# Attention and a Mish MLP on one core: the two row sums of a step are handled one column at a time, and the written-out order is replaced

## The chip, the core and the metric

The kernel runs on one core of a Trainium2 chip. The metric is device time in microseconds (us), the median of several executions. The engines are named as a profile names them: PE is TensorE (matmuls; PEld are its weight loads), DVE is VectorE, ACT is ScalarE, POOL is GpSimd, SP is SyncE, which only starts transfers (DMAs) here. Each works through a queue of its own, in order, and waits for the others by semaphores.

## What is computed

Attention with rotary position embedding over 4 batches of 8 heads, 576 positions, 64 channels, then an MLP with the mish function over all 2304 tokens (512 to 2048 to 512 channels):

```python
scores = scale * np.matmul(q_rot, k_rot.transpose(0, 1, 3, 2))
scores = scores - np.max(scores, axis=-1, keepdims=True)
attn = np.exp(scores)
attn = attn / (np.sum(attn, axis=-1, keepdims=True) + 1e-09)
x = np.matmul(attn, v).transpose(0, 2, 1, 3).reshape(2304, 512)
h = x @ w_in
g = h * np.tanh(np.where(h > 20.0, h, np.log1p(np.exp(np.minimum(h, 20.0)))))
out = g @ w_out
```

## The kernel before

Two heads are a pair P (0 to 15); four pairs are a batch. A pair's 576 query rows are done in steps t of 128 rows, and step 4 of an even pair takes the last 64 rows of two pairs, so there are 72 steps. One step (`step`, L577) runs as follows. `scores` (L475) multiplies on PE into two PSUM pairs, one for each head. `max_exp` (L504) takes the row maximum on DVE (L507) and on ACT the exp with the sum of each row into a column of `sm` (L509): `sm` has two columns, one for each head. `inverse` (L514) adds 1e-9 to both sums and scales them (L517, one instruction over two columns), and takes the reciprocal (L519) into `rs`. The first 18 steps (batch 0, the exact ones) turn e on PE (`turned`, L534: transposes L542, L557, L559, copied out by ACT or DVE). The other 54 steps write weights in two fp16 parts (L523, L525 or L526, on POOL, ACT or DVE; L530 on DVE, which reads e and the first part) and turn them by a DMA on SP's queue. `av` (L606) multiplies by V and leaves the result in two parts in `xt` (L660 to L665).

The rotation of q and k (`rope_turn`, L367) is two multiplies and an add a half tile (L383, L387), on POOL but for the first pair, where DVE shares it. The MLP's weights come as fp64 words and are decoded into two fp16 parts (`decode`, L742: L751 to L771, on ACT, POOL and DVE), after their largest exponent was found (`amax`, L718, and `max_exponent`, L336: a maximum on DVE, L340, a transpose on PE, L343, a maximum, L345, two small operations, L333, a broadcast on PE, L349). The MLP runs in eight chunks of 256 or 320 tokens: `h_unit` (L856; matmuls L873, mish L878), `h_split` (L882; L888 or L889, then L892) and `p_sub` (L896; matmuls L909, eviction L917 or L918, store).

The order of all this is not found when the program is built: `ORDER` (L59) lists every operation by its number in the plan, and each engine's queue is that list's rows for that engine. A letter behind the number (b, c) picks the second or third engine that an operation may run on; `@` gives its PSUM banks; `+n` puts n fills ahead of it (L1022: matmuls of the identity matrix with itself into a bank that is about to be overwritten, which compute nothing and keep PE busy). The durations written in the calls of `op` serve the search that made the list; when the kernel is built they have no effect. In batch 0 ahead of the first MLP product the weights of w_in are decoded beside the steps; the first such product (L873) stands behind pair 3's second step.

Of the kernel before, what the change touches and what calls it, by code (L numbers as in the profile page):

```python
# [18 lines left out]
ALU = mybir.AluOpType  # L19
# [40 lines left out]
    59 58 3 5 2 11 6 4 92 137b 108 20 107 119 32 109 131c 12 7 110@0 19 8b 111 112 113 114@1+3 13 115 116 14 118@2 9  # L60
    15 159 136@3 10b 125b 120 64@45+10 25 23 124@0 138 45 121 63 21 65 62 67 66 156 16b 68 139 130@1 78@45+5 69 24 126
    70 22 132 71@2 79 26 72 38 81 80 61 75@3+6 158 60 82 29 157 140 85@4+5 127 27 86 133 73@2+4 77 201b 170 141 28 134
    93@54+5 160 122 17b 169 76 195b 123 87@0 33 83 171 88 94 172@1 30 161@3 189b 173 84 95 174 42 96 89@0+4 175 162 97
    176@1 163 135 177 117 128 164 142@54+3 98 178 229 194@3 129 74 165@1 196 90 91 224@2 39 166 180 145 188@0 181 143
    183b 517 146 228 43 144 40 225 240b 190 151@4+4 36 447 200@1 230 168 191 231@2 41 232 34 192 147 202 149@0 152 148
    203 150 102@5 37 233 182@2 197 35 234 204 279 235@0+5 100@1 103 193 51 198 210@45 184 46 101 236 99 199 237 291b
    185 104@3 239@0 211 153@1 186 205 280 105 212 187 213 106 349 154 155 281 214 448 282@2+12 348 52 251@3 265@45+3
    241 518 246b 215 283 226 242 219@1 18 47 284 266 245@2 330@0 252b 268 267 53 247 269 285 253 49 220 216 217@4 248
    270 48 331 272@1 218 254 44 274@2 54 50 271 369 286@0 275 258 316@54 449 273 368 55 257@3 243 221@2 319 244 222
# [12 lines left out]
    701 645@1 811 495 696 475@4 496 482 818 490 497 477 491 498 478 890@3 492b 646 516 574@54 891 807 481@0 855b 894
    1077 473 819 577 483 578 816@1 748 624 484 575 814@3 895 576 479b 856 606@45 815 535 480 1078 607 817 538 608 892b
    539@0 583@3 540 893 581@1 609 1104 541 610 542 485b 579 543@0 486 582 611 627@45 580 544 584 545 1105b 546 474 626
    1106 585@1 628 698 561@0 821 613@3 700 630 629 1107@2 563 631 547 586b 697 548 564 615@4 614 1120 556c 555@0 499
    550c 718 616 632 557 565 1121 558 549@5 566 587b 751 634@3 551 1147 612 636 633 822 552 567@0 705 820 730b 653@45
    635b 559 553b 944 1148b 554 617@1 656 640@3 654 657 560 1150@2 702 655 642b 569 618 619 669@54 570 641b 571b 637@1
    572 670 699 1163 638 639b 647 672 947 643 671 752 766@0 658 704 602 673 648 736c 948 694 644b 703 945 706 674 659
    707@1 767 676@5 946 744 708 662@3 677 709 675 710 660@0 573 605 663b 1014 711@1 661 754@45 750 712 768b 713 769
    714 678@3 717@1 757 1164 1149 719 679 715 720 724b 664@0 1017 755 729@3 1202 665b 756 666b 731 1015 758 680@1 732  # L90
    1203 759 772@45 723@0 681b 716 1204 725 682 800@3 733 721b 760 775 735@2 762 773 722 737 774 726 1016 776 1205@1
    738 727 777 741 734b 761b 788@45 739b 835 728b 778 740 801 1218 780b 791 802 764 779b 859 1219 803 792 763 1242
    863 789 1018 765 790 896@0 781 860 782 1243 823@54 793 839 861 742 794 864 795b 865 898@2 862 796b 826 867 783 824
    827 798 918@3 825 899 797 828 840 842@45 829 866 830 919 868 938@1 1165 897 836 971 916 845 799 869 843 914@2 831
    939 844 832 870@3 833 932@0 871 837 846 872 873 917 1019 967 874@1 878@45 834 875 975 933b 934 847 961@3 972 879
    876 881 880 848 942@1 882 968b 849c 962 850 900@4 851 883 976 969 884 990@0 943 852 901 877 973 915 853 963 902@54
    1020b 974 940 886c 965@3 964 1083 885b 854 941 992 903 970 1012@1 1244 966 905 991 906 1010b 935@2 1079 993 1122
    887 904 1166b 1057@3 888 1013 1011 889 920@45 1167b 936 907 743 1168 908 1058 1180 1036@0 910b 921 923 922 1084
    1293 937 1040@1 1080b 909c 924 1008@3 912 1041 911 949@45 925 1085 1294 913 841 1125 926 1037 1187 994@2 952 1009
    1059 928c 1061 950 1123 1245@1 927b 995 1060 951 1261 1062 1038b 929 1054@0 838 953 930 1039 931 978@45 954 1124  # L100
    955 957b 1262 1086 981 956b 979 1280 958 1276 980 1297 959 982 1055 983 996@45 960 1081 1277b 984 977 985 1278
    1279@3 997 986b 1126 999 998 0 987 1320 1000 1184 1087 1281 988 1021@45 1001 1082 1056 1002 1033@2 1024 1004b 1022
    1025 1003 1023 1005 989 1042@54 1026 1006 1181 1027 1321 1043 1029b 1028 1045 1044 1031 1007 1334 1046 1088 1047
    1030 1064@54 1335 1048 1282b 1034 1089 1050b 1032 1337@1 1283 1067 1065 1298 1363 1066 1068 1049c 1295 1052
    1092@54 1336 1051 1169 1127 1069 1364 1128b 1053 1070 1093 1072b 1071 1095 1377 1094 1073 1096 1074 1108@54 1097
# [174 lines left out]
def attention_mish_mlp(ctx: ExitStack, tc: tile.TileContext, qk, v, vflat, rope, ident_in, w_in, w_out, outT):  # L280
# [42 lines left out]
    def tiny(out, r, fn):  # L323
        op((DVE, 110, fn), w=[out], r=r)
        return out
# [761 lines left out]
```

## Time and profile before

| | us |
|---|---|
| median of 3 executions | 624.96 |
| lowest, highest | 623.92, 626.55 |
| the profiled execution, its time | 625.7 |
| its span, first to last instruction | 623.9 |
| PE busy in it | 592.5 |
| DVE, ACT, POOL busy | 460.6, 400.5, 236.4 |

The profile shows one execution. Busy time is the time in which an engine worked on at least one instruction; matmuls are pipelined and a single one lasts longer than the distance to the next, so counts times durations are more than busy time. A row of a timeline gives an instruction's start and length; instructions of DVE overlap a little at their ends. The two totals of a stretch that are compared below are its length and an engine's busy time in it.

### The profile page before, as it was taken

What the parts mean: (1) busy time and instruction counts of PE and PEld (TensorE: products, weight loads), DVE (VectorE), ACT (ScalarE), POOL (GpSimd) and SP (SyncE); (2) the same over time, 40 slices, a digit from 0 to 9 for tenths busy, and PEclk for the clock granted to TensorE, in tenths of its full rate; (3) what the DMA queues carried; (4) which work ended last, traced back from release to release, by engine and by line L of the source; (5) the groups of instructions that cost most, each with busy time, mean ns of one, the idle gap of its engine ahead of it and who ended that gap; (6) DMA issues with size and microseconds to landing.
All of it is one profiled execution on the core that took longest, in us unless ns stands there. A gap on an engine that the chain in (4) does not pass through costs nothing. (4 is left out here: it accounts for less than half of the span.)

```text
span 623.9 us, 12751 instructions
## 1 busy us (share of the span) xinstructions
PE 592.5 (95%) x5065; PEld 440.5 (71%) x5065; DVE 460.6 (74%) x897; ACT 400.5 (64%) x774; POOL 236.4 (38%) x214
## 2 busy tenths in 40 slices
PE   3888899898999999999999999999999999999997
PEld 2555576676666656788887767888777778887775
DVE  5899998999989989948798977686778862520210
ACT  3699888685779776578769844587599544302420
POOL 2798576556463435453362471365100300000000
PEclk9999899999999999999999999999999999999999
DMA  9976123423498599944793677624562662500000
GB/s 342 407 288 255 71 69 128 140 80 116 105 246 178 118 184 223 236 62 92 142 253 88 143 134 175 128 70 92 94 119 43 126 117 58 87 9 9 10 20 32
DMA packets 143435, 82.48 MB, mean 132 GB/s; under 512 B 128144, under 2 KB 133904, under 8 KB 141712
## 3 DMA queue, kind: packets, MB, share of 16 engines
q1 hardware_dynamic: 138768, 76.95, 50.8%
q10 hardware_dynamic: 4608, 4.72, 2.3%
q8 instruction: 39, 0.64, 0.4%
q14 instruction: 20, 0.16, 0.1%
HBM read 45.09 MB, written 4.72 MB: 80 GB/s over the span
## 5 line engine op out<-in xcount | busy, mean ns | idle before, releaser
L873 PE MATMUL bank<-xt,w 128*128 128x320 f16 (+1 forms) x1392 | 181.1, 286 | 0.2 <-DVE xt L665 0.2
L909 PEld LDWEIGHTS <-w 128*128 128x128 f16 x1536 | 146.9, 98 | 46.3 <-issue 9.0
L873 PEld LDWEIGHTS <-w 128*128 128x128 f16 x1536 | 148.1, 98 | 43.3 <-issue 7.1
L909 PE MATMUL bank<-g,w 128*128 128x320 f16 (+1 forms) x1344 | 176.5, 288 | 0.0
L509 ACT ACTIVATE e<-pair,mx 128x576 f32<-128x576 f32 x144 | 105.8, 738 | 57.7 <-DVE mx L507 34.1
L507 DVE TENSOR_REDUCE mx<-pair 128x1 f32<-128x576 f32 x144 | 104.4, 747 | 19.4 <-PE pair L499 19.1
L383 POOL TENSOR_TENSOR raw<-raw,cs 128x576 f32<-128x576 f32 (+2 forms) x61 | 90.7, 1499 | 44.3 <-DMA raw<-in_qk 37.2
L530 DVE SCALAR_TENSOR_TENSOR ew<-e,rs,ew 128x576 f16<-128x576 f32 x108 | 100.7, 946 | 2.4 <-ACT ew L525 2.2
L892 DVE SCALAR_TENSOR_TENSOR g<-mh,cells,g 128x640 f16<-128x640 f32 (+1 forms) x56 | 51.1, 926 | 52.6 <-ACT g L888 52.4
L499 PE MATMUL pair<-qk 64*128 64x288 f32 (+1 forms) x704 | 87.0, 372 | 2.0 <-ACT e L509 1.3
L878 ACT ACTIVATE mh<-bank,cells 128x256 f32<-128x256 f32 (+1 forms) x116 | 55.2, 499 | 44.8 <-PE bank L873 38.5
L523 POOL TENSOR_SCALAR ew<-e,rs 128x576 f16<-128x576 f32 x29 | 24.7, 855 | 130.2 <-DVE rs L519 70.1
L499 PEld LDWEIGHTS pair<-qk 64*128 64x128 f32 (+1 forms) x704 | 55.7, 185 | 23.5 <-issue 11.5
L525 ACT ACTIVATE ew<-e,rs 128x576 f16<-128x576 f32 x49 | 37.5, 770 | 24.1 <-issue 16.0
L517 DVE TENSOR_SCALAR sm<-sm 128x2 f32<-128x2 f32 x72 | 29.5, 410 | 20.1 <-ACT e L509 20.1
L638 PE MATMUL bank<-et,v 128*64 128x256 f16 (+1 forms) x288 | 39.8, 288 | 0.0
L639 PE MATMUL bank<-et,v 128*64 128x256 f16 (+1 forms) x288 | 39.8, 288 | 0.0
L638 PEld LDWEIGHTS <-v 128*64 128x64 f16 x288 | 29.6, 110 | 8.4 <-issue 5.7
L878 ACT ACT_TABLE_LOAD x26 | 33.4, 1283 | 3.0 <-DVE rs L519 1.6
L509 ACT ACT_TABLE_LOAD x25 | 32.1, 1283 | 2.0 <-DVE mx L507 1.6
L387 POOL TENSOR_TENSOR raw<-raw 128x288 f32<-128x288 f32 x32 | 31.1, 980 | 0.9
L918 DVE TENSOR_SCALAR ot<-bank,cells 128x320 f32<-128x320 f32 (+1 forms) x19 | 9.8, 515 | 28.0 <-PE bank L909 19.5
(148 smaller groups left out, 754.7 us busy)
## 6 DMA issues: line engine op xcount, KB each, us to landing
raw<-in_qk SPq DMA_DIRECT2D x30, 576.0 KB, 4.8
w<-in_w_out SPq DMA_DIRECT2D x5, 1024.0 KB, 5.0
g<-in_w_in SPq DMA_DIRECT2D x4, 1024.0 KB, 6.1
w<-in_w_in SPq DMA_DIRECT2D x4, 1024.0 KB, 8.6
stg<-in_v SPq DMA_DIRECT2D x8, 320.0 KB, 4.5
out_dram<-ot ACTq DMA_DIRECT2D x16, 160.0 KB, 2.1
stg<-in_vflat SPq DMA_DIRECT2D x6, 384.0 KB, 3.9
qk<-in_w_out SPq DMA_DIRECT2D x4, 512.0 KB, 6.0
```

Of the source, the lines that this page charges most:

```text
L383: e.tensor_tensor(out=t()[:, :, s], in0=t()[:, :, s], in1=cs()[:, :, s], op=ALU.mult)
L499: nc.tensor.matmul(pts[h]()[to, c, :HS], x[own, q], y[own, s], **kw)
L507: op((DVE, dve_ns(S), lambda: nc.vector.tensor_reduce(m(), pt()[:, :, :HS], axis=AX.XY, op=ALU.max, negate=True)), w=[m], r=[pt])
L509: op((ACT, act_ns(S, psum=True, ptr=2), lambda: nc.scalar.activation(e().rearrange("p (c s) -> p c s", c=2), pt()[:, :, :HS], AF.Exp, bias ...
L525: (ACT, act_ns(S, ptr=1), lambda: nc.scalar.activation(w()[:, c], e(), AF.Copy, scale=r()[:, h:h + 1])),
L530: op((DVE, dve_ns(S) + 180, lambda: nc.vector.scalar_tensor_tensor(out=w()[:, c], in0=e(), scalar=r()[:, h:h + 1], in1=w()[:, hc], op0=ALU ...
L638: nc.tensor.matmul(po()[0:64, :n], V()[:, vi, c, 0:64], et[:, c, :], start=False, stop=last)
L639: nc.tensor.matmul(po()[64:128, :n], V()[:, vi, c, 64:128], et[:, 5 + c, :], start=False, stop=last)
L873: nc.tensor.matmul(hp(), w1()[:, wi, cc, f:f + 128], x()[:, xi, cc, q0:q0 + n], start=cc == 0 and a == 0, stop=cc == NCC - 1 and a == 2)
L878: op((ACT, act_ns(n, psum=True, ptr=1) + 40, lambda j=j, hp=hp: nc.scalar.activation(hn()[:, j, :n], hp(), AF.Mish, scale=uh())), w=[(hn, ...
L892: op((DVE, dve_ns(2 * n) + 61, lambda: nc.vector.scalar_tensor_tensor(out=gv()[:, 1, f, :n], in0=hn()[:, :, :n], scalar=f32(gs), in1=gv()[ ...
L909: nc.tensor.matmul(pp()[:, :n], w2e[e]()[:, wi, f], gv()[:, gi, f % 4, :n], start=f == 0 and a == 0, stop=f == NF - 1 and a == 2)
```

## The change

The add on the row sums becomes two instructions of one column each. `ORDER` is replaced by a new list, found again by the same kind of search after some of the durations written in the code were changed; the list has 2368 operations where it had 2296, 72 of them the added adds. Of the table two lines stand here for all:

```diff
-    59 58 3 5 2 11 6 4 92 137b 108 20 107 119 32 109 131c 12 7 110@0 19 8b 111 112 113 114@1+3 13 115 116 14 118@2 9
+    59 2 58 3 5 11 6 4 20 140b 111 12 134c 94 122b 110 128b 19 112 113@0+16 32 7b 114 115 116 117@1+7 118 13 119 9
...
     def inverse(sm, n, scale=2.0 ** -15):
         r = sbuf((128, 2), F32, "rs", 3)
-        both = [(sm, h) for h in range(n)]
-        op((DVE, 125, lambda: nc.vector.tensor_scalar(sm()[:, 0:n], sm()[:, 0:n], 1e-9, scale, op0=ALU.add, op1=ALU.mult)),
-           w=both)
-        op((DVE, 135, lambda: nc.vector.reciprocal(r()[:, 0:n], sm()[:, 0:n])), w=[(r, h) for h in range(n)], r=both)
+        for h in range(n):
+            op((DVE, 85, lambda h=h: nc.vector.tensor_scalar(
+                sm()[:, h:h + 1], sm()[:, h:h + 1], 1e-9, scale, op0=ALU.add, op1=ALU.mult)), w=[(sm, h)])
+        op((DVE, 100, lambda: nc.vector.reciprocal(r()[:, 0:n], sm()[:, 0:n])),
+           w=[(r, h) for h in range(n)], r=[(sm, h) for h in range(n)])
         return r
```

Nine other durations in the calls of `op` are changed with nothing else on their lines. In the new file the lines behind the table stand three lower, and four lower from the reciprocal on (L520 is the add, L522 the reciprocal, L722 and L759 are the old L718 and L755).

What the new list does to the counts: fills 77 to 124 (ahead of the first scores 13 to 48: 16, 7 and 25 in three groups, then groups of 14 and 16); on DVE, apart from the adds, L755 on w 3 to 0, casts L768 11 to 6, L552 10 to 5, L889 on g of 640 columns 9 to 19; on ACT L767 up by five, L888 on g of 640 columns 23 to 13, table loads 51 to 47. The rough order of PE's work, step by step and chunk by chunk, stays.

The first place is DVE's queue at the add of pair 2's first step. Before, one add (on `sm`) stands eight rows ahead of its reciprocal:

```order
L686 TENSOR_REDUCE cells_66<-raw_370 128x1
L757 SCALAR_TENSOR_TENSOR bank0_73<-bank0_73,w2_68 128x512
L517 TENSOR_SCALAR sm_451<-sm_451 128x2
L345 TENSOR_REDUCE cells_66<-bank2_75 1x1
L760 SCALAR_TENSOR_TENSOR w2_68<-w2_68,bank0_73 128x512
L333 TENSOR_SCALAR cells_66<-cells_66 1x1
L507 TENSOR_REDUCE mx_503<-pair0_77 128x1
L507 TENSOR_REDUCE mx_516<-pair1_78 128x1
L757 SCALAR_TENSOR_TENSOR bank2_75<-bank2_75,w2_68 128x512
L333 TENSOR_SCALAR cells_66<-cells_66 1x1
L757 SCALAR_TENSOR_TENSOR bank3_76<-bank3_76,w2_68 128x512
L519 RECIPROCAL rs_531<-sm_451 128x2
```

Now the two adds of that step stand four rows apart, and the reciprocal three rows behind the second:

```order
L761 SCALAR_TENSOR_TENSOR bank2_75<-bank2_75,w2_68 128x512
L355 COPY cells_66<-bank0_73 128x1
L520 TENSOR_SCALAR sm_502<-sm_502 128x1
L764 SCALAR_TENSOR_TENSOR w2_68<-w2_68,bank2_75 128x512
L761 SCALAR_TENSOR_TENSOR bank1_74<-bank1_74,w2_68 128x512
L661 TENSOR_TENSOR ew_484<-bank3_76,ew_484 128x256
L520 TENSOR_SCALAR sm_502<-sm_502 128x1
L764 SCALAR_TENSOR_TENSOR w2_68<-w2_68,bank1_74 128x512
L722 TENSOR_REDUCE cells_66<-w2_68 128x1
L522 RECIPROCAL rs_608<-sm_502 128x2
```

What moved: the row of two columns became two rows of one, the first of them placed ahead of a decoding step and an eviction.

The second place is SP's queue at the start of the program, which only starts loads. Before (`g` holds the first quarter of w_in, `cs` the rotation's tables, `raw` q and k of pair 0, `ident` the identity matrix that PE's transposes and fills read):

```order
L705 DMA g1_82<-in_w_in 128x1024
L705 DMA g0_84<-in_w_in 128x1024
L1003 DMA cs_64<-in_rope 128x2x320
L374 DMA raw_87<-in_qk 128x2x320
L1001 DMA ident_65<-in_ident 128x128
L374 DMA raw_90<-in_qk 128x2x320
L374 DMA raw_87<-in_qk 128x2x256
L1003 DMA cs_64<-in_rope 128x2x256
L449 DMA v16_94<-in_v 128x640
```

Now:

```order
L709 DMA g1_82<-in_w_in 128x1024
L1005 DMA ident_65<-in_ident 128x128
L709 DMA g0_85<-in_w_in 128x1024
L1007 DMA cs_64<-in_rope 128x2x320
L377 DMA raw_88<-in_qk 128x2x320
L377 DMA raw_90<-in_qk 128x2x320
L377 DMA raw_88<-in_qk 128x2x256
L1007 DMA cs_64<-in_rope 128x2x256
L380 DMA raw_94<-in_qk 128x1152
```

What moved: the identity matrix went from the fifth place to the second; pair 1's k came ahead of pair 0's last half of q and of v.

The third place is DVE's queue ahead of the maximum (L340, now L343) of w_out's last quarter, for which PE's transpose L343 (now L346) waits. Before:

```order
L552 COPY et_1508<-bank1_74 128x4x64
L507 TENSOR_REDUCE mx_1597<-pair0_77 128x1
L832 TENSOR_SCALAR cells_66<-cells_66 128x1
L517 TENSOR_SCALAR sm_1544<-sm_1544 128x2
L718 TENSOR_REDUCE cells_66<-raw_1418 128x1
L665 SCALAR_TENSOR_TENSOR xt0_69<-ew_1077,cells_66,xt0_69 128x320
L755 TENSOR_SCALAR raw_1217<-raw_1217 128x512
L572 COPY ew_1624<-bank3_76 128x64
L718 TENSOR_REDUCE cells_66<-qk_1580 128x1
L340 TENSOR_REDUCE cells_66<-cells_66 128x1
```

Now:

```order
L759 TENSOR_SCALAR raw_1486<-raw_1486 128x512
L510 TENSOR_REDUCE mx_1677<-pair0_77 128x1
L572 COPY et_1600<-bank3_76 128x64
L556 COPY et_1600<-bank0_73 128x4x64
L722 TENSOR_REDUCE cells_66<-qk_1478 128x1
L520 TENSOR_SCALAR sm_1660<-sm_1660 128x1 x2
L821 TENSOR_SCALAR cells_66<-cells_66 128x1
L520 TENSOR_SCALAR sm_1615<-sm_1615 128x1
L722 TENSOR_REDUCE cells_66<-qk_1644 128x1
L576 COPY ew_1490<-bank3_76 128x64
L343 TENSOR_REDUCE cells_66<-cells_66 128x1
L661 TENSOR_TENSOR ew_1490<-bank2_75,ew_1490 128x320
```

What moved: the decoding instruction on raw (L755, now L759) stood three rows ahead of that maximum and stands ten ahead of it; L665 (now L669), two tiles from SBUF, stood between and is now behind.

## Rows read from the trace of the kernel before

**Rows 1.** the page's totals: busy us, share of the span, instructions.

```profile
PE 592.5 (95%) x5065; PEld 440.5 (71%) x5065; DVE 460.6 (74%) x897; ACT 400.5 (64%) x774; POOL 236.4 (38%) x214
```

**Rows 2.** busy us by stretch; stretch (us), its length, engines, clock, DMA.

```profile
core 0: us, PE busy (x) PEld busy (x) DVE busy (x) ACT busy (x) POOL busy (x), PEclk, DMA share, GB/s
10.00:78.00 68.00, 58.71 (x391) 38.16 (x392) 63.88 (x140) 54.82 (x123) 51.03 (x50) 0.97 0.70 267
78.00:150.00 72.00, 67.71 (x569) 49.70 (x567) 69.14 (x162) 54.05 (x109) 46.62 (x42) 1.00 0.31 105
150.00:270.00 120.00, 115.95 (x961) 80.23 (x962) 108.21 (x213) 88.72 (x173) 57.56 (x53) 1.00 0.84 180
270.00:380.00 110.00, 109.68 (x1023) 84.82 (x1021) 92.66 (x159) 79.71 (x146) 47.63 (x39) 1.00 0.59 127
```

**Rows 3.** PE's timeline at the start: start, us, engine, line, operation, tiles, count, idle.

```profile
10.20 0.37 PE L343 MATMUL bank<-ident,cells 128*1 128x128 f32 x1 [10.20 <-DMA ident<-in_ident]
11.92 2.32 PE L1022 MATMUL pair<-ident 128*128 128x256 f16 x10
14.16 2.29 PE L499 MATMUL pair<-qk 64*128 64x288 f32 x8
25.64 0.60 PE L1022 MATMUL bank<-ident 128*128 128x256 f16 x4
27.58 1.24 PE L499 MATMUL pair<-qk 64*128 64x288 f32 x8 [0.35 <-ACT qk L395]
```

**Rows 4.** PE's waits from 78 to 270 us: total us, times, longest.

```profile
PE bank L634 <- DMA et<-ew: 3.1, 3, 1.2
PE bank L343 <- DVE cells L340: 2.4, 2, 1.8
PE bank L626 <- DVE cells L333: 1.1, 1, 1.1
PE bank L349 <- DVE cells L333: 0.6, 2, 0.4
```

**Rows 5.** all instructions of lines 517 and 333: ns min/median/max, first, last, forms.

```profile
L517 DVE TENSOR_SCALAR sm<-sm x72: 149/169/1385, 19.1 to 523.4; 128x2 f32<-128x2 f32 x72
L333 DVE TENSOR_SCALAR cells<-cells x66: 126/141/214, 11.0 to 500.4; 128x1 int32<-128x1 f32 x21, 128x1 int32<-128x1 int32 x16, 1x1 int32<-1x1 int32 x12, 1x1 f32<-1x1 int32 x12
```

**Rows 6.** DVE's timeline around one add.

```profile
48.34 1.25 DVE L517 TENSOR_SCALAR sm<-sm 128x2 f32<-128x2 f32 x1
50.31 0.13 DVE L333 TENSOR_SCALAR cells<-cells 1x1 int32<-1x1 int32 x1
50.37 1.40 DVE L507 TENSOR_REDUCE mx<-pair 128x1 f32<-128x576 f32 x2
```

**Rows 7.** POOL's timeline in the same stretch.

```profile
46.52 3.06 POOL L383 TENSOR_TENSOR raw<-raw,cs 128x640 f32<-128x640 f32 x2
49.52 0.88 POOL L387 TENSOR_TENSOR qk<-raw 128x320 f32<-128x320 f32 x1
```

**Rows 8.** line 517 alone, by stretch: length, busy us and count on DVE.

```profile
0.00:78.00 78.00, 4.79 (x8) 0.98 0.72 272
78.00:270.00 192.00, 12.46 (x29) 1.00 0.64 152
270.00:624.00 354.00, 12.26 (x35) 1.00 0.44 91
```

**Rows 9.** DVE's timeline around another add.

```profile
64.01 1.13 DVE L517 TENSOR_SCALAR sm<-sm 128x2 f32<-128x2 f32 x1
65.05 1.45 DVE L665 SCALAR_TENSOR_TENSOR xt<-ew,cells,xt 128x256 f16<-128x256 f32 x1
```

**Rows 10.** DVE's timeline at 147 us, then line 755 on w: ns min/median/max.

```profile
147.35 1.76 DVE L755 TENSOR_SCALAR raw<-raw 128x512 int32<-128x512 int32 x1
...
L755 DVE TENSOR_SCALAR w<-w x3: 416/419/887, 111.5 to 134.4; 128x512 int32<-128x512 int32 x3
```

**Rows 11.** the page's groups: ScalarE's table loads, count, busy, mean ns.

```profile
L878 ACT ACT_TABLE_LOAD x26 | 33.4, 1283 | 3.0 <-DVE rs L519 1.6
```

More of the change, by code (lines that the diff above doesn't have):

```diff
@@ L65 @@
[L65 to L69, printed above, removed]
@@ new lines @@
+    359 390 362 304 360 311 614 368@5 305 393@0 455 366@3 369 395 1 456 418@45 340 306 457 31 396 261 367 526@1 419
+    411@2 307 421 420 635@0 210 363 243 422 413 211 527 414 667@4 312b 183 301b 426@3 550 313 636 546@2 268 471 364
+    668 472 365 388 423 405@1 609 549 606@5 415 407 547 408 703@0 607 212 665b 399@2 701b 666 409 435@45 427b 410 704
+    318 401 370@1 436 610 684@0 372 397 371b 402 416 437 213 438 428@3 825@1 615 429b 766 702 439 806@2 398b 826 424
+    618 441 440 511@45 442 425 709 434 685 789@3 514 807 403 269 833b 430@1 804b 790 319b 449@0 515 431b 404 432b
@@ new lines @@
+    1720 1678 1487 1444 1445 1679@4 1732 1671 1777@3 1680 1698 1578 1682 1488 1454@54 1778 1725 1486 1735@0 1455 1579
+    1726 1733@2 1582 1446 1419 1736 1728 1457 1447 1729@3 1734 1456 1779b 1448c 1752@0 1420 1780 1421 1458 1787@1 1449
+    1730 1450 1491@54 1788 1753 1789@2 1494 1750b 1495 1492 1783@3 1460 1459 1751 1493 1504@1 1497 1785b 1461 1784
+    1496 1462 1498 1463c 1464 1513@45 1451 1500b 1620 1790 1781@0 1514 1499c 1786 1825@3 1782 1823b 1672 1465 1333
+    1515 1826 1502 1466 1516 1501 1526@2 1517 1824 1821b 1547@45 1519 1518 1527 1503 1822 1505 1506 1583 1827 1520
@@ new lines @@
+    2270b 2251 2308@1 2263 2271 2278@0 2260@4 2273 2261 2259 2268b 2279 2269 2274 2300@5 2275 2280 2276b 2277 2309
+    2284@2 2301 2281 2326@3 2282 2285 2302@1 2296@4 2303 2320@0 2297 2290@1 2306@5 2291 2307 2286 2310b 2298@4 2287
+    2299 2316 2292 2304 2317 2283 2311 2324@5 2293 2325 2288b 2305 2289 2312@4 2321 2330@2 2313 2327 2294 2318@0
+    2314@3 2319 2334 2295 2338@1 2328 2315 2322b 2332@0 2323 2335 2350@3 2329 2339 2351 2344@1 2336@5 2345 2337 2333
+    2331 2346 2340b 2342b 2341 2352 2343 2347 2353 2348b 2349 2356@0 2357 2354b 2355 2358 2359 2362@2 2360b 2361 2363
@@ L162 @@
+    2364 2365 2366 2367
 """
@@ L323, in tiny @@
     def tiny(out, r, fn):
-        op((DVE, 110, fn), w=[out], r=r)
+        op((DVE, 90, fn), w=[out], r=r)
         return out
@@ L463, in load_v @@
             (DVE, dve2_ns(640), lambda: nc.vector.tensor_copy(o()[:, 0], tv()), 1)], w=[(o, 0)], r=[t])
-        op((POOL, pool_ns(640), lambda: nc.gpsimd.tensor_tensor(out=o()[:, 1], in0=tv(), in1=o()[:, 0], op=ALU.subtract), 1),
+        op((POOL, pool_ns(640) + 180, lambda: nc.gpsimd.tensor_tensor(out=o()[:, 1], in0=tv(), in1=o()[:, 0], op=ALU.subtract), 1),
            w=[(o, 1)], r=[t, (o, 0)])
@@ L508, in max_exp @@
            w=[m], r=[pt])
-        op((ACT, act_ns(S, psum=True, ptr=2), lambda: nc.scalar.activation(
+        op((ACT, act_ns(S, psum=True, ptr=2) + 35, lambda: nc.scalar.activation(
             e().rearrange("p (c s) -> p c s", c=2), pt()[:, :, :HS], AF.Exp, bias=m(), accum_out=sm()[:, h:h + 1])),
@@ L529, in weights_lo @@
     def weights_lo(w, part, hpart, c, hc, e, r, h):
-        op((DVE, dve_ns(S) + 180, lambda: nc.vector.scalar_tensor_tensor(
+        op((DVE, dve_ns(S) + 130, lambda: nc.vector.scalar_tensor_tensor(
             out=w()[:, c], in0=e(), scalar=r()[:, h:h + 1], in1=w()[:, hc], op0=ALU.mult, op1=ALU.subtract), 1),
@@ L754, in decode @@
             (ACT, act_ns(512), lambda: nc.scalar.activation(*bits(), AF.Copy, scale=LOW, bias=-0.4999)),
-            (DVE, 410, lambda: nc.vector.tensor_scalar(
+            (DVE, 570, lambda: nc.vector.tensor_scalar(
                 get()[:, :, 0], get()[:, :, 0], 29, None, op0=ALU.logical_shift_right))], w=[low], r=[whole])
```

192 lines of the change are left out of this document (92 added, 100 removed).

## The prediction

> **What bounds the kernel now.** I read the page's totals first. TensorE (PE) is busy 592.5 us of 623.9 [rows 1], so only 31.4 us can be had from waits as long as no product is dropped, and the change drops none. The table by stretch says where they lie [rows 2]: 10 to 78 us has 58.7 us of 68.0 busy (9.3 idle), 78 to 150 has 67.7 of 72.0 (4.3), 150 to 270 has 115.95 of 120.0 (4.05), 270 to 380 only 0.3. The rest is the start (the first matmul waits 10.2 us for the identity matrix [rows 3]) and about 3.4 us of the last eviction and store. So behind 270 us PE alone sets the end and no other engine's gain counts; ahead of it VectorE (DVE) is as full as PE or fuller: 63.9 of 68.0, 69.1 of 72.0, 108.2 of 120.0 [rows 2]. In the first stretch PE's own busy time holds the fills, matmuls that compute nothing, so DVE is the bound there; in the next two PE is nearly full and waits at single places. The list of PE's waits from 78 to 270 us names them [rows 4]: 3.1 us for transposing DMAs, and 2.4, 1.1 and 0.6 us for small DVE results.
>
> **Part 1, the add.** The add on a step's two row sums (L517, 128x2) lasts 149 to 1385 ns with a median of 169, while 66 one-column operations of the same kind (L333) last 126 to 214 and never more [rows 5]. The long ones have a neighbour: the one at 48.34 us lasts 1.25 us, to 49.59, and GpSimd (POOL)'s pair of multiplies ends at 49.58 [rows 6, 7]. So a two-column add waits until POOL's running instruction is done, with DVE's queue standing behind it; nothing of L333's shape does. By stretch, the 72 adds take 4.79 us (8 of them, up to 78 us), 12.46 us (29, from 78 to 270) and 12.26 us (35, later) [rows 8]. At 0.16 each unhindered they would take 1.28, 4.64 and 5.60, so 3.5, 7.8 and 6.7 us of waiting are freed.
>
> The price is one more instruction a step. A one-column operation lasts 0.13 us at 50.31, but the next instruction starts at 50.37, 0.06 later [rows 6]. I take 0.06 from that row, with 0.14, a full duration, as the upper bound: 8 x 0.06 to 8 x 0.14 = 0.5 to 1.1 us up to 78 us, 29 x 0.06 to 29 x 0.14 = 1.7 to 4.1 from 78 to 270. The Trainium skill speaks against the change here: "VectorE: DVE Perf Modes", section "The DRAIN you can't avoid", holds that the next operation does not start before the pipe is empty, and the page's rules ask to minimize the count of operations. By that rule each added add would cost its full 0.14, 2.4 and 3.7 us would be freed in the two stretches instead of 3.0 and 6.1, and the sum below would come out about 1.5 us higher, near 620.5; the row at 50.37 disagrees with it for this shape. An added wait: the first column can be added once the first head's exp is done, so DVE may stop twice a step, and what is queued behind it (a row maximum that ScalarE's exp waits for) stops too. Most of the 72 pairs stand one to four rows apart, and the second add waits for what the old one waited for, so I price it at nothing; its cover is that the first head's exp ends one exp ahead of the second's.
>
> Net on DVE: 3.5 - 0.5 = 3.0 us (2.4 at the other price) up to 78 us, 7.8 - 1.7 = 6.1 us (3.7) from 78 to 270, and some 4.5 us later, where it is worth nothing.
>
> What of it reaches the end: from 10 to 78 us DVE is idle for only 4.1 us [rows 2], so nearly all should; I take 2.5, between 0 and 3.0, because after one long add (64.01) the next instruction waits for POOL in its turn [rows 9].
>
> **Part 2, the order from 78 to 270 us.** PE is idle 4.3 + 4.0 = 8.3 us there [rows 2], and no gain can be more. The longest wait (1.8 of the 2.4 us for L340) follows DVE's L755 on raw at 147.35, which took 1.76 us where the same form on w has a median of 0.42, and which stands three rows ahead of the maximum that PE waits for [rows 4, 10]. In the new order it stands ten rows ahead, with both reductions between, so I count this 1.8 as gone; what is late next is the last reduction itself. Of the other waits I count 1.7: those on L333 (1.1 and 0.6) hang on DVE's queue, which gets 6.1 us shorter. The 3.1 us for the transposes stays in the sum, although they are issued behind DVE's last instruction of a step. Together 3.5, bounds 0 and 8.3. Nothing below zero comes from the waits removed; what a new order can add is the rival with the sign against.
>
> The moves between engines: three L755 and five casts of decoded weights leave DVE, ten g splits join it (these late, behind 270 us, at no cost); ScalarE takes the casts, and loses four table loads at 1.28 us each [rows 11]. ScalarE is 54.05 of 72.0 busy from 78 to 150, so eight moved instructions of some 0.7 us lie within its 18 us of idle time. I cost these at nothing; if that cover is gone (ScalarE's exps queue behind the casts), PE's waits for e grow, by up to 8 x 0.7 = 5.6 us.
>
> **Part 3, the start.** The identity matrix's load goes from fifth to second on SP's queue, behind 1 MB instead of some 2.7 MB by the tiles' shapes; the loads it passes move back by its 64 KB, some 0.2 us. PE can then run fills from about 6 us, and the fills grow from 77 to 124, 48 of them ahead of the first scores where 13 stood. Ten fills took 2.32 us at 11.92, four 0.60 at 25.64; a block of scores 2.29 at 14.16 and 1.24 at 27.58 [rows 3]: the same work in half the time once PE has been busy for a while. If the earlier fills bring that forward to the first scores, the two blocks of the first pair save 2 x 1.05 = 2.1 us. If not, 25 fills at 0.23 are 5.8 us from about 11.7, and the first scores, ready at some 14.2 to 15 in either kernel, start near 17.5: 3.3 us late. Bounds -2.1 and +3.3; I take 0, since the 23 fills ahead of the 25 are some five us of earlier work for PE, which speaks for the first end, and 25 in a row are more than the gap needs, which speaks for the second.
>
> **Sum.** The profiled execution took 625.7 us, 1.8 outside its span. 625.7 - 2.5 - 3.5 + 0 = 619.7. It lies 0.7 above the median of 624.96, so against the median I expect 619.0.
>
> **Rivals.** (a) The freed wait is handed on. POOL's instruction still runs, and the next DVE operation that reads two SBUF tensors waits for it instead: right after the long add at 64.01, L665 took 1.45 us [rows 9]. The Trainium skill, "SBUF — State Buffer", section "Who interferes with whom", has such a rule: a DVE instruction with two SBUF inputs contends with a GpSimd one that reads SBUF; the trace agrees at this row. For it: every step behind the first eighteen has two L530 of that kind. Against it: the long adds at 48.34 and at most others up to 150 us are followed by instructions that read PSUM or one tensor and start at once. If it holds, and the new order only shuffles PE's waits, part 1 gives 1.0 and part 2 1.0: 623.0, within half a percent. (b) Slower: the fills. If the 25 ahead of the first scores run at 0.23 each, the first pair starts 3.3 us late, every row maximum behind it with DVE idle, and the next 14 and 16 can add a further 1 to 3 us between the first transposes. With part 1 and 2 at nothing: 625 + 3.3 to 6 = 628 to 631. It decides once the first scores start behind 16.7 us. Against it: 23 fills run before. (c) The one-column add still waits for POOL, so that the change doesn't do what it says: a step then has two such waits, and up to 78 us as much as 3.5 us is lost instead of won, 628. The 66 of L333 without a long one speak against it [rows 5]; chance 0.02.
>
> **How the numbers follow.** The forecast (a gain of over 3.1 us, half a percent, about what a measurement of this kernel can tell) gets 0.61, (a) and its like 0.25, (b) and (c) 0.14. The low end takes all of PE's waits from 78 to 270 (8.3), 3.0 from part 1 and 2.1 from the start: 624.96 - 13.4 = 611.6, and I write 611.5. The high end takes the gain at nothing and part of (b): 627. Less than 2 in 10 is left out.
>
> **What would show it.** Right: no one-column add over 0.22 us; the first h product (L873), at 77.5 us now, some 2 to 3 us earlier; PE idle from there to the middle 4 us instead of 8; the stretch behind unchanged. Part 3 shows in the start of the first scores (14.16 now) and in whether that block takes 1.24 or 2.29. Wrong: L530, L665 and L526 longer by what the adds lost, or PE's waits for e, qk and et grown, or PE idle behind the first fills.

## The result and the profile after

The changed kernel takes 614.89 us in the median (614.16 to 616.05, 5 runs) against 624.9 (623.88 to 626.55, 5 runs): a ratio of 0.9843, 95% interval [0.9822, 0.9865]. A second session gave it 615.77 (615.03 to 616.5, 6 runs) beside 626.0 of the kernel before, 0.9834 [0.9808, 0.9859]. So it is faster by 10 us where 6.0 were forecast (2.5 and 3.5); the forecast's sign and its range hold, and one of its terms was too small. Single executions of one kernel differ, in part by stretches at half clock (each of the two traces read here has one of 3.4 us), so medians are compared with medians, and the traces place by place. In the changed kernel the line numbers are 3 higher up to the reciprocal, which is now L522, and 4 higher behind it.

The page's totals of the changed kernel answer to [rows 1]: PE does 47 matmuls more, all of them fills, in the same busy time, and the span is 613.7 us instead of 623.9.

```profile
PE 592.6 (97%) x5112; PEld 442.8 (72%) x5112; DVE 447.2 (73%) x964; ACT 390.9 (64%) x771; POOL 239.9 (39%) x218
```

All instructions of the add, ns min/median/max, answer to [rows 5] and [rows 8]: none is over 0.155 us.

```profile
L520 DVE TENSOR_SCALAR sm<-sm x144: 129/143/155, 20.1 to 511.6; 128x1 f32<-128x1 f32 x144
```

Busy us by stretch, with the columns of [rows 2]: DVE is idle for 7.5 us from 78 to 150 us where it had 2.9, and PE is idle for 1.3 there instead of 4.3. ScalarE has taken 7.7 us of work there and still has 10.3 free. (The stretches are the same times, so those of the changed kernel hold work of some 6 us later.)

```profile
10.00:78.00 68.00, 62.48 (x475) 44.01 (x476) 65.42 (x168) 58.83 (x131) 57.44 (x55) 0.97 0.71 268
78.00:150.00 72.00, 70.72 (x603) 51.36 (x603) 64.55 (x171) 61.72 (x128) 45.51 (x43) 1.00 0.36 117
150.00:270.00 120.00, 116.53 (x994) 81.95 (x991) 103.17 (x213) 86.23 (x170) 64.57 (x56) 1.00 0.81 175
270.00:380.00 110.00, 109.81 (x1017) 83.78 (x1015) 87.93 (x182) 70.22 (x134) 36.09 (x30) 1.00 0.68 138
```

PE's waits from 78 to 270 us (total us, times, longest) answer to [rows 4]: the waits on maxima (2.4, of it 1.8 on the last one) are gone, those on L333 are 1.1 instead of 1.7, a new one of 0.8 waits for a load of w_out, and the transposing DMAs cost 2.1 instead of 3.1.

```profile
PE bank L638 <- DMA et<-ew: 2.1, 2, 1.5
PE bank L352 <- DVE cells L336: 1.1, 1, 1.1
PE bank L913 <- DMA w<-in_w_out: 0.8, 1, 0.8
PE bank L546 <- DVE ew L661: 0.2, 1, 0.2
PE bank L638 <- issue: 0.2, 1, 0.2
```

PE's timeline at the start answers to [rows 3]: fills from 6.05 us, the first scores at 14.66 and in 1.24 us.

```profile
6.05 3.47 PE L1026 MATMUL bank<-ident 128*128 128x256 f16 x16 [6.05 <-DMA ident<-in_ident]
...
11.28 2.90 PE L1026 MATMUL pair<-ident 128*128 128x256 f16 x25
14.66 1.24 PE L502 MATMUL pair<-qk 64*128 64x288 f32 x8 [0.48 <-DVE qk L390]
```

Where the 10.2 us between the two spans lie: the first h product starts at 71.70 us (77.49 before), 5.8 earlier. From there to the last matmul PE stands idle for 5.3 us (8.7 before), 3.3 less; its blocks of work are 1.4 us shorter, 0.9 of that in score blocks, some of which had waited inside for a buffer (L502 is busy for 76.6 us from there on, L499 for 77.5 before); the tail is 0.3 longer.

### The profile page after: what moved, and what is told of

Same layout as the page of the kernel before. It is cut to its first block, busy times and chain, and to the rows that moved or that the text cites. A ratio compares the mean times of both kernels' runs of the same rounds, so it can differ in the third digit from the quotient of the medians.

```text
span 613.7 us, 12945 instructions
## 1 busy us (share of the span) xinstructions
PE 592.6 (97%) x5112; PEld 442.8 (72%) x5112; DVE 447.2 (73%) x964; ACT 390.9 (64%) x771; POOL 239.9 (39%) x218
## 5 line engine op out<-in xcount | busy, mean ns | idle before, releaser
L877 PE MATMUL bank<-xt,w 128*128 128x320 f16 (+1 forms) x1284 | 166.8, 286 | 0.1
L386 POOL TENSOR_TENSOR raw<-raw,cs 128x576 f32<-128x576 f32 (+2 forms) x62 | 94.3, 1538 | 74.3 <-DMA raw<-in_qk 70.3
L534 DVE SCALAR_TENSOR_TENSOR ew<-e,rs,ew 128x576 f16<-128x576 f32 x108 | 104.8, 988 | 4.5 <-ACT ew L529 3.4
L502 PE MATMUL pair<-qk 64*128 64x288 f32 (+1 forms) x704 | 84.2, 366 | 1.1 <-ACT e L512 0.5
L527 POOL TENSOR_SCALAR ew<-e,rs 128x576 f16<-128x576 f32 x33 | 27.0, 819 | 146.2 <-DVE rs L522 79.8
L882 ACT ACTIVATE mh<-bank,cells 128x320 f32<-128x320 f32 (+1 forms) x107 | 50.5, 498 | 37.7 <-PE bank L877 25.1
L502 PEld LDWEIGHTS pair<-qk 64*128 64x128 f32 (+1 forms) x704 | 54.3, 181 | 21.5 <-issue 10.1
L893 DVE TENSOR_SCALAR g<-mh,cells 128x640 f16<-128x640 f32 (+1 forms) x32 | 16.9, 533 | 51.3 <-ACT mh L882 35.5
L529 ACT ACTIVATE ew<-e,rs 128x576 f16<-128x576 f32 x44 | 33.7, 769 | 15.5 <-issue 9.8
L882 ACT ACTIVATE mh<-pair,cells 128x256 f32<-128x256 f32 (+1 forms) x21 | 10.4, 495 | 36.8 <-PE pair L877 31.8
L877 PE MATMUL pair<-xt,w 128*128 128x256 f16 (+1 forms) x252 | 33.9, 284 | 0.0
```

What stands on the lines that cost most here:

```text
L386: e.tensor_tensor(out=t()[:, :, s], in0=t()[:, :, s], in1=cs()[:, :, s], op=ALU.mult)
L502: nc.tensor.matmul(pts[h]()[to, c, :HS], x[own, q], y[own, s], **kw)
L529: (ACT, act_ns(S, ptr=1) + 25, lambda: nc.scalar.activation(w()[:, c], e(), AF.Copy, scale=r()[:, h:h + 1])),
L534: op((DVE, dve_ns(S) + 130, lambda: nc.vector.scalar_tensor_tensor(out=w()[:, c], in0=e(), scalar=r()[:, h:h + 1], in1=w()[:, hc], op0=ALU ...
L877: nc.tensor.matmul(hp(), w1()[:, wi, cc, f:f + 128], x()[:, xi, cc, q0:q0 + n], start=cc == 0 and a == 0, stop=cc == NCC - 1 and a == 2)
L882: op((ACT, act_ns(n, psum=True, ptr=1) + 60, lambda j=j, hp=hp: nc.scalar.activation(hn()[:, j, :n], hp(), AF.Mish, scale=uh())), w=[(hn, ...
```

## The experiments

Two kernels that issue the same matmuls in the same order can be laid over each other: fills left out, the n-th matmul of one stands against the n-th of the other. This table, worked out from the traces, gives the lead (-) or lag (+) in us of the second kernel, at the first matmul past the given time of the first one. Each figure comes from one execution of each kernel. The two runs of the changed kernel (fourth line) show how far the same code wanders: up to 1.2 us, so a figure of that size elsewhere counts only with a row that shows where it comes from. e4's front has another order of matmuls, so its line starts at 78 us. The executions fall into three sessions (the first result aside), e1 to e4, e5 to e8 and e9 to e12, each on another chip; ratios are to the kernel before in the same session.

```
second against first              30    55    78   100   150   170   210   239   300   end
e1 against before               -1.0  -2.8  -5.1  -5.9  -6.5  -6.5  -6.1  -6.0  -6.2  -6.9
e2 against after, 2nd run       +0.3  +1.8  +2.3  +2.3  +4.0  +3.0  +3.7  +6.0  +6.1  +5.8
e4 against after, 2nd run                   +1.8  +2.0  +3.9  +2.5  +3.6  +2.9  +4.2  +4.1
after, 1st against 2nd run      -0.1  +0.9  +1.1  +1.0  +1.1  +1.2  +1.2  -0.2  +0.8  +0.4
e6 against after, 2nd run       +0.7  +0.8  +0.8  +0.8  +1.3  -0.2  +0.9  -0.4  +0.1  +0.1
e9 against e1                   -0.3  -0.3  +0.6  +0.6  -1.1  -1.4  -1.6  -1.7  -2.0  -2.0
e11 against before              -0.1  -0.1  -1.3  -1.2  -1.2  -1.2  -1.2  -1.1  -1.0  +1.0
e12 against e7                  -0.4  -0.6  -0.3  -0.1  +1.2  +1.3  +1.1  +1.9  +1.9  +1.4
```

**e1 to e4, the parts alone.** e1 has the new add and the old order, with the second add's row right behind the first's. e2 has the new order, with one two-column add where the second one stands:

```
+        seen = []
...
+        def add():
+            seen.append(1)
+            if len(seen) == n:
+                nc.vector.tensor_scalar(sm()[:, 0:n], sm()[:, 0:n], 1e-9, scale, op0=ALU.add, op1=ALU.mult)
         for h in range(n):
-            op((DVE, 85, lambda h=h: nc.vector.tensor_scalar(
-                sm()[:, h:h + 1], sm()[:, h:h + 1], 1e-9, scale, op0=ALU.add, op1=ALU.mult)), w=[(sm, h)])
+            op((DVE, 85, add), w=[(sm, h)])
```

> The order of the kernel before, with each two-column add replaced by two one-column adds in the same place (adjacent). Theory A (the freed wait for POOL carries much of the gain): no add over 0.22 us, the first h product some 2 to 3 us ahead of 77.5, the end 3 to 5 us ahead of before: 620 to 622. Theory B (the new order carries it, and a freed wait is handed on to the next DVE instruction): 623.5 to 625.5, with L530, L534 and L669 longer by what the adds lost.

> The new order, with one two-column add at the place of a step's later add and nothing at the place of the earlier one. Theory A: the adds wait for POOL again, about as often as before (some 15 us in all), and about 3 to 5 us of the 10 are lost: 618 to 620. Theory B: 614.5 to 616.

Measured: e1 619.26 us (618.78 to 620.11), 0.9888 [0.9858, 0.9919]; e2 622.52 (619.05 to 627.05, 11 runs; a twelfth took 628.41), 0.995 [0.9919, 0.998]. The add alone is worth 6.7 us, the order alone some 3 (e2's runs spread over 8 us, and the interval goes from 1.3 to 5.1), together about as much as the change. Both are on the side of theory A and beyond it: e1 gains 5.1 us at the first h product where 2 to 3 were expected and ends below 620, and e2 loses some 7 where 3 to 5 were. In e1 DVE's busy time falls by 11.7 us: 13.4 less in the adds (29.5 to 16.1 us), 2.4 more in the 108 subtractions of L530, now L534 (100.7 to 103.1 us). A pair of one-column adds on DVE in e1 (start, us) takes 0.12 until the next instruction starts, 0.06 for each:

```profile
46.21 0.21 DVE L520 TENSOR_SCALAR sm<-sm 128x1 f32<-128x1 f32 x2
46.33 0.27 DVE L348 TENSOR_REDUCE cells<-bank 1x1 f32<-1x128 f32 x1
```

In e1 and in the changed kernel no add waits although POOL works beside it: 42 and 52 of the 144 one-column adds began while a POOL instruction had over 0.25 us still to run, and none took over 0.157 us. In the kernel before 25 of the 72 two-column adds began so; all 25 were long (0.33 to 1.39 us) and ended 0.02 to 0.03 us behind POOL's instruction, which carries the reading of [rows 6] and [rows 7] from one add to all.

The table's first line says where the gain arises: 1.0 us by 30 us, 2.8 by 55, 5.1 by the first h product, 1.4 more by 150 and, on balance, 0.4 after that. The first 1.0 is not the adds': the first long add of the kernel before starts at 32.1 us. It comes with PE's clock, full from 24.3 us before and from 21.4 in e1; the same four transposes, first before, then in e1:

```profile
21.54 1.11 PE L542 MATMUL bank<-ident,e 128*128 128x128 f32 x4
```

```profile
21.58 0.66 PE L546 MATMUL bank<-ident,e 128*128 128x128 f32 x4
```

Why it rises earlier is open (e4, with the same front as e1, has it at 21.3 us, e11, with that of before, at 23.8). From 30 to 55 us the adds waited 2.5 us, 2.2 net of the added ones, and 1.8 are gained; from 55 to 78 two adds give back only 0.9 net, and 2.3 are gained. Two timelines of PE show where the 1.4 more come from, first the kernel before, where PE stands for 1.36 us behind the long add of [rows 9], the clock then falls to half from 68.7 to 72.1 us, and a score block takes 2.14 us:

```profile
66.64 0.44 PE L559 MATMUL pair<-ident,rs 128*64 128x128 f32 x4 [1.36 <-DVE rs L519]
...
68.74 1.06 PE L542 MATMUL bank<-ident,e 128*128 128x128 f32 x4
69.73 0.58 PE L349 MATMUL bank<-ident,cells 1*128 1x1 f32 x2
70.25 2.14 PE L499 MATMUL pair<-qk 64*128 64x288 f32 x8
```

and the same matmuls in e1, where the clock stays full:

```profile
62.44 0.44 PE L563 MATMUL pair<-ident,rs 128*64 128x128 f32 x4 [0.51 <-DVE rs L522]
...
64.52 0.60 PE L546 MATMUL bank<-ident,e 128*128 128x128 f32 x4
65.05 0.38 PE L352 MATMUL bank<-ident,cells 1*128 1x1 f32 x2
65.35 1.25 PE L502 MATMUL pair<-qk 64*128 64x288 f32 x8
```

The table's second line is the price of the two-column add in the new order: 2.3 us in the front, 3.7 from 78 to 239, nothing later. Of the last part some 1.5 us is once more half clock, from 238.7 to 242.1 us, behind a wait of 1.5 for an exp: 0.6 in the score block below, which takes 1.96 in the second run at full clock, and 0.9 in the products behind it (PE in e2):

```profile
237.43 2.53 PE L496 MATMUL pair<-qk 64*128 64x288 f32 x8 [1.50 <-ACT e L506]
```

e3 and e4 have one-column adds and a seam in the order: its first 391 rows from the one order, the others from the other.

> One-column adds; the first 391 operations in the new order (up to the first h product, with the new start), the rest in the old one. If the gains of the two stretches add up, the first h product starts at 71.7 as in the changed kernel and the end lies 5.4 to 6 ahead of before plus what the one-column adds give the rest (some 2 us): 617 to 619.5. If the rest can't use the earlier start (DVE is full there), 621 or more.

> One-column adds; the first 391 operations in the old order with the old start, the rest in the new one. If the gains add up: the first h product at 74.5 to 75.5 (the adds alone), the end at 617.5 to 619.5. If the new order's gain behind 78 us hangs on the new front, 621 or more.

Measured: e3 619.61 us (617.38 to 622.71), 0.9896 [0.986, 0.9932]; e4 620.43 (619.08 to 621.37), 0.9904 [0.9872, 0.9936]; both lie between the two times that were named for them. Neither half gains anything over e1, though the whole gains 4. So the halves don't add up, and these two runs give no price for either: by the table's third line e4, with the new rest behind the old front, is 1.8 us late at 78 us and 4.1 at the end. (The profiled execution of e3 has half clock from 39.6 to 46.5 us, and its order of matmuls is that of neither kernel, so it is not in the table.)

**e5 to e8, one session.** e5 is the changed kernel unedited, told of above and called its second run.

> The changed kernel once more, nothing edited, as the yardstick for the three runs beside it. Both theories: about 614.9 us, the first h product at 71.7 us. The profile tells whether the stretch of half clock at 40.0 to 43.4 us comes again in a second execution.

Measured: 615.77 us; the first h product at 70.63 instead of 71.70, and no half clock in the front. A score block of PE tells the difference, first in the first run (half clock from 40.0 to 43.4 us), then in the second:

```profile
39.78 2.73 PE L502 MATMUL pair<-qk 64*128 64x288 f32 x8
```

```profile
39.88 1.69 PE L502 MATMUL pair<-qk 64*128 64x288 f32 x8
```

The 1.1 us last until 210 us and are gone at 239: from 205 to 245 us PE waits 2.2 us on products behind transposes (L638) in the second run and 0.8 in the first. At the end 0.4 is left.

e6 undoes part 3. The order's rows name operations by number, with the fills behind a plus sign:

```
-    59 2 58 3 5 11 ... 113@0+16 ... 117@1+7 ... 64@45+25
+    59 58 3 5 2 11 ... 113@0    ... 117@1+3 ... 64@45+10
```

> The changed kernel with the start of the kernel before: the identity matrix is loaded fifth again, and 0, 3 and 10 fills stand ahead of the first three products where 16, 7 and 25 stood; all else as changed. My part 3 was taken at 0: then 614.9 within 1 us and the first h product at 71.7 within 0.5. If the early fills are worth what the clock record suggests (full from 9.3 us and not from 24.3), the first scores take 2.29 us again in place of 1.24, and the first h product and the end come 1 to 2 us later: 616 to 617. If the fills were a loss, 613 to 614.

Measured: 615.18 us (614.25 to 617.41), 0.9826 [0.9799, 0.9854]. The first scores take 2.29 us again (row below), the first h product is 0.8 late, and at the end 0.1 of that is left in the trace and nothing in the median: on L638 PE waits 0.8 us from 160 to 245, where the second run waits 3.6.

```profile
14.99 2.29 PE L502 MATMUL pair<-qk 64*128 64x288 f32 x8 [0.85 <-DVE qk L390]
```

e7 fills three gaps ahead of 40 us:

```
-    236@2   ... 105@3   ... 240@0
+    236@2+4 ... 105@3+2 ... 240@0+4
```

> The changed kernel with ten more fills in three places where PE stood idle: 4 ahead of the transpose at 37.05 us (idle 0.58), 2 ahead of the transposes at 37.71 (0.39), 4 ahead of the product at 39.47 (0.52). Theory A: the clock falls to half at 40.0 because PE stood idle before, and the half clock is paid for (the block of scores at 39.78 took 2.73 us where 1.25 is usual, and DVE waited 1.0 us behind it): with the gaps filled the record stays full, the scores take 1.25, the first h product comes 1 to 1.5 us earlier and the end with it, 613.5 to 614. Theory B: something else holds the front (the first h product came at 72.3 to 72.4 in three kernels with different fronts): the clock may stay full, but the first h product moves by less than 0.3 us and the time stays at 614.9.

Measured: 614.52 us (614.1 to 615.1), 0.9813 [0.9785, 0.984]. The profiled execution has a full clock, but so has that of e5, and the first h product (70.52) agrees with e5's, so the traces don't tell theory A from theory B. The times of one session do differ: five of e7's six lie below all six of e5's (615.03 to 616.5), and the median is 1.2 us lower, though only 0.4 lower than that of the first session. It fits theory A that the mean granted clock is 0.999 or 1.0 in all six executions of e7, while five of the eleven of the changed kernel have 0.993 to 0.997; but e6 and e10, without these fills, also have 0.999 or 1.0 in all six. So e7 is about 1 us faster in its own session, and the cause isn't shown.

e8 is e2 with the two sums in columns 0 and 2 of a tile of three, where the exps write them and the reciprocal reads them (against e2, the add alone):

```
-                nc.vector.tensor_scalar(sm()[:, 0:n], sm()[:, 0:n], 1e-9, ...)
+                nc.vector.tensor_scalar(sm()[:, 0:3:2], sm()[:, 0:3:2], 1e-9, ...)
```

> The changed order with one add for both sums of a step again, at the place of the second one-column add, but the two sums lie two elements apart (a tile of three columns, first and third used). It asks what the wait for POOL hangs on. Theory A: on the number of elements a partition (two): the adds take up to 1.4 us as with the pair side by side, and the time is that of the order alone, about 622. Theory B: on the two lying side by side: no add is over 0.25 us, the kernel has 72 instructions less than the changed one, and the time is 614 to 615, perhaps 1 us below it up to where DVE is full.

Measured: 621.72 us (620.09 to 623.17), 0.9925 [0.9897, 0.9952], theory A, 6.0 us above the changed kernel in the same session: the price of the two-column add in the new order. Two columns that don't touch wait as two that do: all 22 adds that began while a POOL instruction had over 0.25 us to run were long (0.33 us and more). The reciprocal on the same two columns never waits, though 14 of the 72 began so (all 72 of each in e8, ns min/median/max):

```profile
L518 DVE TENSOR_SCALAR sm<-sm x72: 146/166/1369, 20.7 to 518.0; 128x2 f32<-128x2 f32 x72
```

```profile
L522 DVE RECIPROCAL rs<-sm x72: 142/156/166, 22.6 to 518.2; 128x2 f32<-128x2 f32 x72
```

**e9 to e12.** e9 is e1 with one letter changed, `754c` to `754b`: the subtraction on raw goes from DVE to ScalarE.

> The old order with one-column adds (as e1), and a single operation moved: the subtraction on raw that stood on DVE at 147.35 us (L755 of the kernel before, 1.76 us) is done by ScalarE, as in the changed kernel. In e1 PE still stood idle for 1.79 us ahead of the product that waits for the maximum three rows behind it. My part 2 (that wait hangs on this operation, 1.8 us, and nothing takes its place): that idle time falls below 0.4, the step that begins at 146.8 us in e1 begins 1.4 to 1.8 earlier, and the end follows: 617.5 to 618 against 619.3 of e1. Rival: the wait is handed on to the next late result (the last reductions of w_out, or ScalarE's queue), the end stays at 619.3 within 0.4.

Measured: 618.25 us (617.19 to 619.91), 0.987 [0.9841, 0.99], 1.0 below e1's median; the two are of different sessions and their intervals overlap, so the traces decide. PE's waits from 78 to 150 us, in e1 and then in e9: the 1.8 is gone and nothing has come in its place.

```profile
PE bank L346 <- DVE cells L343: 1.8, 1, 1.8
PE bank L630 <- DVE cells L336: 1.1, 1, 1.1
PE bank L352 <- DVE cells L336: 0.9, 1, 0.9
PE pair L502 <- ACT e L512: 0.5, 1, 0.5
```

```profile
PE bank L630 <- DVE cells L336: 1.1, 1, 1.1
PE bank L352 <- DVE cells L336: 0.9, 1, 0.9
PE pair L502 <- ACT e L512: 0.5, 1, 0.5
```

In the table e9 gains 1.7 us between 100 and 150. The two waits on L336 (L333 of before) stay, although DVE is rid of the long adds.

e10 gives the late steps their two-column add back:

```
...
+            if not late or len(seen) == n:
+                c = slice(0, n) if late else slice(h, h + 1)
+                nc.vector.tensor_scalar(sm()[:, c], sm()[:, c], 1e-9, scale, op0=ALU.add, op1=ALU.mult)
...
-        r = inverse(sm, 2, 1.0 if exact else 2.0 ** -15)
+        r = inverse(sm, 2, 1.0 if exact else 2.0 ** -15, P >= 9)
```

> The changed kernel, but the 31 steps of the pairs from 9 on (from about 289 us to the end) get their two-column add back, at the place of the second one-column add; the 41 steps ahead of them keep one-column adds. My step that DVE's gain behind 270 us is worth nothing: the long adds (up to 1.4 us) return there and DVE's busy time grows by some 4 us, but the time stays at 615.8, within 0.6, as in the second run of the changed kernel. Rival (the whole freed time counts, wherever it lies): 3 to 4 us slower, 619.

Measured: 614.36 us (613.97 to 615.76), 0.981 [0.978, 0.984]: nothing lost. But the edit took hardly anything back. The groups of the add in e10 (count, busy us, mean ns): the adds of the 31 late steps take 7.8 us, 0.25 each; only three of them were long, waiting 2.9 us in all. From 284 us on the adds take DVE 8.1 us, and 8.3 in the second run, with about twice as many; DVE's busy time is 446.5 us, not some 4 above 447.2. So e10 doesn't decide between its two expectations.

```profile
L525 DVE TENSOR_SCALAR sm<-sm 128x1 f32<-128x1 f32 x82 | 10.4, 142 | 1.1 <-ACT e L512 1.1
L525 DVE TENSOR_SCALAR sm<-sm 128x2 f32<-128x2 f32 x31 | 7.8, 253 | 4.2 <-ACT e L512 4.2
```

e11 is the kernel before with fills around the stand of 1.36 us (`327@4` to `327@4+11`, `458@2` to `458@2+2`).

> The kernel before with 13 more fills and nothing else: 11 ahead of the transposes at 64.84 us, behind which PE stood idle for 1.36 us, and 2 ahead of the product at 67.95. It asks for the cost of the half clock at 68.7 to 72.1, behind that idle time. Theory A: the half clock cost the front 1.8 us that my first term had not counted (the scores at 70.25 took 2.13 us in place of 1.25): with it gone the first h product comes at 75.6 to 76 instead of 77.5 and the end 1 to 1.8 us earlier, less by as much as the executions of the kernel before are without that stretch anyway. Theory B: the wait on DVE is what holds the front: the clock may stay full, but the first h product stays at 77.5 within 0.4.

Measured: 627.74 us (625.34 to 629.34, 12 runs) beside 625.58, 1.0017 [0.9995, 1.0039]: no gain, and by the medians 2.2 us more. In the profiled execution the clock is full and the first h product starts at 76.22, 1.3 us earlier. The table keeps this lead until 300 us; from there to 375 it loses 2.0, half of it in this wait of PE (78 us to the end) on a product behind a transpose, for which the profile shows no cause:

```profile
PE bank L634 <- issue: 0.9, 1, 0.9
```

e12 is e7 without the 36 adds of the exact steps:

```
-            op((DVE, 85, lambda h=h: nc.vector.tensor_scalar(
+            op((DVE, 85, lambda h=h: scale == 1.0 or nc.vector.tensor_scalar(
```

> The changed kernel with the ten fills of e7, and without the add in the 18 steps of the first four pairs, where it adds 1e-9 to a sum that is at least 1 and multiplies by 1: 36 one-column operations less, all in the part of the run where DVE is full or nearly so. At my price of 0.06 us each that is 1.0 us up to the first h product (16 of them) and 1.2 us more up to about 150; since DVE is idle for some 3 us up to there, I expect the first h product 0.5 to 1 us earlier than in e7 (70.5) and the end at 613.3 to 614.2 against 614.5. At the full duration of 0.14 it would be twice that: 612.5 to 613.3. If PE is the bound by now: 614.5.

Measured: 616.06 us (614.51 to 616.54), 0.9827 [0.9799, 0.9855], 1.5 above e7 (of another session) where 0.3 to 1.2 below it was expected. The first h product starts 1.4 us earlier (69.16), and most of that is lost within the h products themselves, because what they multiply isn't ready (PE's waits from 69 to 82 us; e7 has none there):

```profile
PE bank L877 <- DVE xt L669: 0.3, 1, 0.3
PE bank L877 <- ACT mh L882: 0.3, 1, 0.3
PE bank L877 <- DVE w L764: 0.2, 1, 0.2
```

So no version clearly beats the changed kernel: e7 and e10 have medians 1.2 and 1.4 us below its second run and 0.4 and 0.5 below its first, and the two runs themselves differ by 0.9.

## Why the prediction was right, and what was mis-sized

**The add.** Right in its working: no one-column add waits, a second one costs 0.06, and the adds give back 13.4 us in e1, where the three net gains of the forecast (3.0, 6.1 and 4.5) make 13.6. The added wait, priced at nothing, cost nothing: DVE stands for 11.9 us ahead of the adds until an exp is done, and stood for 20.1 before. The prediction read "VectorE: DVE Perf Modes", section "The DRAIN you can't avoid", of the Trainium skill as a rule by which each added operation costs its full duration; the same paragraph adds that a next operation which is not held back starts earlier, and the row at 46.21, with two adds in 0.12 us, agrees with that. Rival (c) is out. Rival (a) holds in small: in e1 the L530 of before is 2.4 us longer (4.1 in the changed kernel, 104.8 us) and the L665 that reads two tiles from SBUF 0.9, together 3.3 of the 13.4, which leaves the forecast's mechanism standing.

**The term that was too small** is the 2.5 us up to 78 us. I bounded it by DVE's own gain, 3.0; e1 gained 5.1 at the first h product, and the changed kernel 5.8. For the adds alone it was about right: 1.8 us from 30 to 55 us, where they give 2.2, and 0.9 from 55 to 78. What it left out is PE's clock: 1.0 us ahead of the first long add, whose cause is open, and 1.4 from 55 to 78, where PE stood for DVE's late result and then ran at half clock. That chain was in the trace of before (1.36 us idle, clock 0.5 from 68.7), but I read only DVE's rows there. e11 takes the half clock away without the add: 1.3 us at the first h product, within the 2.3 that e1 gains from 55 to 78.

**The order from 78 to 270 us.** The sum of 3.5 fits, half of it by luck: PE's idle time behind the first h product fell by 3.3 (2.6 in the second run), nearly all of it there. The 1.8 behind raw is shown by e9 (1.7). What the forecast says of that place is not quite what was done: of the two subtractions on raw the one three rows ahead of the maximum went to ScalarE, as in e9, and the other came to DVE, where it stands ten rows ahead and takes 0.42 us. The long one looks like a further wait for POOL: it ends at 149.11 us, 0.28 behind POOL's multiply (148.83), but no run tests that. The other 1.7 had the wrong cause: I let the waits on L333 shrink because DVE's queue gets shorter, and in e1 and e9 those ahead of 150 us stand at 1.1 and 0.9 with the adds cured. It is the new order that removes these two; with one of 1.1 behind 150 us the changed kernel has 0.6 less on L333 than before, and the rest of the sum came from waits that I had let stand (the transposing DMAs 1.0, the other maximum 0.6, exps 0.6), less 0.8 for the new wait on w_out. What the cured adds do bring in the middle (1.4 us by 150 us in e1, some 3.7 in the new order by e2) came partly from where I looked for nothing, score blocks that wait inside for a buffer and so count as busy. The moves between engines cost PE nothing that shows, as taken: the changed kernel has no wait of PE for e from 78 to 270 us.

**The start.** 0 was right at the end (e6), the lower bound right for the first scores (14.66, 1.24 us); rival (b) did not come to its point of 16.7. The early fills bring 0.8 us at the first h product, which later waits take back.

**Behind 270 us** DVE's gain is worth little or nothing. e10 doesn't show it, as said, but the table's first line bounds it: all long adds are gone in e1, and from 239 us to the end it gains 0.9, less than the same code wanders.

**What stays open.** The two halves of the new order have no price of their own (e3, e4). A lead in the front reaches the end in e1 (5.1, then 6.9) but not in e6, e11 and e12 (0.8, 1.3 and 1.4); places where the smaller leads went are seen (h products whose inputs aren't ready, products behind transposes), but not why the waits behind transposes, around 235 us and past 340, come out as they do.

## What to carry to other kernels

A tiny operation can be the dearest in a queue: look at the maximum of a group, not at its median, and if the long ones end when another engine's instruction ends, change the shape of the operation (here one column for two) before moving it. When such a wait is taken away, follow it into the engine that waits for its result and into that engine's clock: here 1.4 of the 5.1 us that e1 gained in the front lay there. A microsecond won early counts only if nothing between it and the end waits for something else; small leads were gone again within 10 to 300 us.

## What the runs showed of the chip

Whether a DVE operation waits for GpSimd here depends on the operation and on its columns, not on whether they touch: two columns of TENSOR_SCALAR wait side by side (up to 1.41 us in e2) and two elements apart (1.37 in e8), one column doesn't (144 times in the changed kernel, 52 of them beside a POOL instruction with over 0.25 us to run, at most 0.155), and RECIPROCAL on two columns doesn't either (72 times, 18 of them so, at most 0.168). The Trainium skill, "VectorE: DVE Perf Modes", section "What auto-detection actually checks", says that an operation with a single source and its destination in SBUF takes both ports if their outermost sizes other than 1 are both even or equal, and names a step only for the 16-bit modes; e8 agrees with that. Why one column and the reciprocal stay out of it no run here shows.

The half clock after idle time on PE is not the same in each execution: the same kernel had it at 40.0 to 43.4 us in one and not in another, with the same gaps ahead of it (0.58, 0.39 and 0.52 us, and 0.59, 0.39 and 0.52). It cost a score block 1.0 us. In the sessions of e1 to e8 the kernel before ranged from 624.0 to 630.4 us (28 runs), with a mean granted clock of 0.986 to 1.0, and the changed kernel from 615.0 to 616.5 (6 runs) with 0.993 to 1.0. That fewer stands of PE make the time steadier fits this, but no run shows it.
